# Chunked attention into a sine MLP on one core: four passes in another order of words, batch 3's loads issued elsewhere, the last output tile cut 384 and 128

## The chip, the core and the metric

The kernel runs on one core of a Trainium2 chip. The time is device microseconds of one execution of the whole program. A core has five instruction streams that run side by side and wait for each other by semaphores: PE (TensorE, matrix products; its weight loads are shown as PEld), DVE (VectorE), ACT (ScalarE), POOL (GpSimd) and SP (SyncE, which here only issues transfers). Each stream works through its instructions in the order in which the program was written, so an instruction that waits holds up all that stand behind it on its engine. ACT, POOL and SP also issue DMA transfers, which then run by themselves.

## What is computed

`reference.py`, cut to what matters. The attention works on chunks of 32 queries that see 16 keys to the left, 8 to the right and 8 memory rows:

```python
# q, k, v: (4, 8, 768, 64); mem_k, mem_v: (4, 8, 8, 64)
for c in range(768 // 32):
    ctx = slice(max(0, 32 * c - 16), min(768, 32 * c + 40))
    k_full = np.concatenate([mem_k, k[:, :, ctx]], axis=2)
    v_full = np.concatenate([mem_v, v[:, :, ctx]], axis=2)
    a = softmax(q[:, :, 32 * c:32 * c + 32] @ k_full.transpose(0, 1, 3, 2) / 8)
    out[:, :, 32 * c:32 * c + 32] = a @ v_full
x = out.transpose(0, 2, 1, 3).reshape(3072, 512)
h = x @ w_in                       # (3072, 2048)
g = h + sin(alpha * h) ** 2 / alpha
return g @ w_out                   # (3072, 512), float32
```

## The kernel before

Matrix operands are bfloat16, sums float32. The four batches (768 tokens each) pass through in five stages. Stage 0 is attention of batch 0; stage n (n = 1, 2, 3) runs the MLP of batch n-1 and, in between and after it, the attention of batch n; stage 4 is the MLP of batch 3. Only stages 1 to 4 differ in the change. One stage is one string of `WORDS`, written out by hand: `Stage.run` takes the words one by one, and the method for a word's first letter (`do_b`, `do_h`, ...) emits its instructions. So a word's place fixes its place on every engine at once, and an engine on which it emits nothing does not see it.

The MLP of a batch has 16 tiles of 128 of the 2,048 hidden columns:

- `b`*t* and `h`*t*: the two halves of tile *t*'s first product, four 384-column matmuls each (line 462) into two PSUM banks; `h` then has ACT take the sine (line 477)
- `q`*t*`A`, `V` or `P`: the square of the sine on ACT (line 482), DVE or POOL (line 485)
- `g`*t*: DVE's finish (line 489), which writes `gT` and gives the two banks back
- `o`*n*: puts the second product of this batch in the queue `feed`, 96 matmuls for six output tiles of 128 tokens; the first two tiles go together in groups of *n* hidden tiles. `f`*n* takes the next *n* of them (line 500, 512 columns each). After a tile's sixteenth, `close` copies it out of PSUM (line 507, ACT and DVE by turns as `e` says) and SP stores it (line 510). What is left at the end is taken in one go.

There are eight banks. `Banks` gives out pairs and singles in the order in which they were given back, so a `b` waits until an earlier tile's `g` has run.

The attention of a batch has eight blocks of 96 queries:

- `s`*jk..*: scores of these blocks (line 419, 16 matmuls of 96 columns for two blocks, 24 for three), then three exponentials each on ACT (line 433)
- `v`*j*: values (line 448, eight matmuls of 65 columns), then DVE's reciprocal and product (lines 387, 388)
- `t`*j* and `T`*j*: the block turned by PE (line 400) and copied to `xT` by DVE or ACT (line 403); `c`*j*: turned by a DMA transpose that SP issues (line 669)
- `V`*bxy*: POOL issues the loads of `v` of batch *b*, heads *x* to *y*-1 (lines 209, 216; float32 in memory, bfloat16 on chip, into buffer *b* mod 2, with the memory rows between); `m`, `H` copy the memory rows (DVE, or eight copies on POOL, line 232)
- `R`*n*: POOL issues the next *n* loads of the next batch's key rows (16, lines 269 and 275) and, after them, query rows (6, line 282); `Z`: SP adds the memory rows; `X`*n*: SP issues the next *n* DMA transposes of these into `kT` (8, line 297) and `qT` (6, line 300). Batches 2 and 3 come this way.
- Batch 1 comes by `dk`, `dq` (one load each), `k`, `l` (turned by PE, line 313) and `K`, `L` (copies, lines 324 and 333)
- `U`, `I`: loads of `w_out` and `w_in`; `Ws`, `We`: one-element sine or exponential on ACT, which brings the function table in ahead of use.

The word method and the queue of the second product:

Of the kernel before, what the change touches and what calls it, by code (L numbers as in the profile page):

```python
# [27 lines left out]
    ),  # L28
    (
# [5 lines left out]
    ),  # L35
    (
# [5 lines left out]
    ),  # L42
    (
# [5 lines left out]
    ),  # L49
    (  # L50
# [3 lines left out]
    ),  # L54
)

# [66 lines left out]
def kernel(  # L123
# [15 lines left out]
    d_model, d_ff = moe_w_in.shape  # L139
# [178 lines left out]
    def copier(eng):  # L318
        return {"A": nc.scalar.copy, "V": nc.vector.tensor_copy, "P": nc.gpsimd.tensor_copy}[eng]
# [176 lines left out]
    def second(i, gT, group=0):  # L496


        def mm(o, s, ft, c0=0, c1=d_model):
            nc.tensor.matmul(  # L500
                o[:, c0:c1], gT[:, ft, P * s:P * s + P], w_out_sb[:, ft, c0:c1],
                start=(ft == 0), stop=(ft == FT - 1),
            )

        def close(o, bs, s, c0=0, c1=d_model):
            o_sb = mlp.tile([P, d_model], F32, name="o_sb", bufs=3)
            copier(state["engines"][state["o"] % len(state["engines"])])(o_sb[:, c0:c1], o[:, c0:c1])  # L507
            state["o"] += 1
            banks.give(bs)
            nc.sync.dma_start(out[S * i + P * s:S * i + P * s + P, c0:c1], o_sb[:, c0:c1])  # L510

        order = []
        if group:
            order = [(s, ft) for h in range(0, FT, group) for s in range(2)
                     for ft in range(h, h + group)]
        order += [(s, ft) for s in range(2 if group else 0, NSUB) for ft in range(FT)]
        held = {}
        for s, ft in order:
            if i == B - 1 and s == NSUB - 1:
                if ft == 0:  # L520
                    for c0 in (0, 256):
                        o, bs = banks.single()
                        for f in range(FT):
                            mm(o, s, f, c0, c0 + 256)
                        close(o, bs, s, c0, c0 + 256)
                yield
                continue
            if ft == 0:
                held[s] = banks.single()
            mm(held[s][0], s, ft)  # L530
            if ft == FT - 1:
                close(*held.pop(s), s)
            yield
# [7 lines left out]
    class Stage:  # L541
# [63 lines left out]
        def do_o(self, a):  # L605
            feed.add(second(self.i, self.gT, int(a)), NSUB * FT, lambda: self.ready(int(a)))
# [244 lines left out]
    def const_s():  # L851
# [4 lines left out]
                     s=const_s, z=const_z)  # L856
# [37 lines left out]
```

## Time and profile before

| | us |
|---|---|
| three runs, median (lowest to highest) | 215.28 (214.47 to 216.2) |
| the profiled execution, its own time | 214.86 |
| its span | 212.7 |
| its granted TensorE clock | 1.0 |

The span is what the trace covers; the rest of the execution's time lies around it. Times in views of the profile are counted from the span's start. The stages stand in the trace as follows: stage 1 begins its MLP at about 23.7 us, stage 2 at 74.2, stage 3 at 120.6, stage 4 at 167.3, and the last stretch of line 500 begins at 189. A line of the groups reads: source line, engine, operation, result and inputs, tile sizes, count, busy time in all, mean ns of one, then the idle time of the engine ahead of these instructions with what ended it. In the chain of waits, a line is a start, a length and the work that the end of the program depended on at that time.

### The profile page before, as it was taken

To read this page: it belongs to the slowest core of one execution; us is meant where nothing else is said; L and a number is where in the kernel's file an instruction comes from. 1 tells how busy PE (TensorE), PEld (TensorE's weight loads), DVE (VectorE), ACT (ScalarE), POOL (GpSimd) and SP (SyncE) were. 2 spreads that over 40 slices of the span, in tenths; PEclk is the share of its full clock that TensorE was granted. 3 is DMA by queue.
4 is the path that set the end of the run, shared out by engine and by line. 5 is a ranking of instruction groups with operands and counts; after the bars stand their busy time and mean duration, and the time that the engine had idled before them with its cause. 6 is when DMAs were issued, how large, how long until landed. Compare 5 with 4: busy or idle time off the path is not lost.

```text
span 212.7 us, 4568 instructions
## 1 busy us (share of the span) xinstructions
PE 203.1 (95%) x1759; PEld 118.0 (55%) x1781; DVE 139.2 (65%) x210; ACT 143.5 (67%) x229; POOL 100.1 (47%) x142
## 2 busy tenths in 40 slices
PE   7799899999999999999999999999999999999994
PEld 7467655655455555554456555554455455554453
DVE  4888788998352669957675569896347187865010
ACT  2698798968838579978827298968755189891110
POOL 8998607497497395129893058582000022200000
PEclk9999999999999999999999999999999999999999
DMA  5999999999999999999997259999944400000312
GB/s 158 328 156 140 210 209 204 204 164 176 166 143 133 180 136 123 114 142 158 140 206 111 90 119 117 151 140 132 130 105 107 136 0 3 2 0 0 151 49 99
DMA packets 95853, 27.82 MB, mean 131 GB/s; under 512 B 84808, under 2 KB 92376, under 8 KB 95832
## 3 DMA queue, kind: packets, MB, share of 16 engines
q0 software_dynamic: 69152, 13.64, 92.4%
q1 hardware_dynamic: 25720, 12.68, 29.6%
q10 hardware_dynamic: 960, 1.21, 1.7%
q8 instruction: 14, 0.23, 0.6%
q14 instruction: 7, 0.06, 0.1%
HBM read 29.66 MB, written 6.29 MB: 169 GB/s over the span
## 4 chain that ended last, share of the span: by engine, by line
PE 72%; DVE 7%; DMA 7%; ACT 6%; issue 4%; POOL 2%; SPq 1%; DVEq 0%
PE ps L500 35%; PE ps L462 28%; DMA vw<-in_v_dram 4%; DVE gT L489 3%; DMA kq_f<-in_k_dram 3%; PE ps L448 3%; DVE s L485 2%; PE ps L419 2%; ACT u L477 2%; DVE x_blk L388 2%; PE ps L313 1%; PE ps L400 1%; ACT s L482 1%; ACT qT L333 1%; POOL vw L209 1%
## 5 line engine op out<-in xcount | busy, mean ns | idle before, releaser
L500 PE MATMUL ps<-w_out_sb,gT 128*128 128x512 bf16 (+1 forms) x382 | 86.9, 370 | 1.3 <-issue 0.3
L462 PE MATMUL ps<-xT,w_in_sb 128*128 128x384 bf16 x512 | 86.2, 326 | 0.7 <-DVE gT L489 0.2
L489 DVE SCALAR_TENSOR_TENSOR gT<-s,inv_alpha,ps 128x768 bf16<-128x768 f32 x64 | 63.0, 1011 | 12.5 <-ACT s L482 5.1
L462 PEld LDWEIGHTS <-w_in_sb 128*128 128x128 bf16 x512 | 49.6, 98 | 35.4 <-issue 2.1
L477 ACT ACTIVATE u<-ps,alpha_sb 128x768 f32<-128x768 f32 x64 | 56.6, 894 | 17.8 <-PE ps L462 15.9
L500 PEld LDWEIGHTS <-gT 128*128 128x128 bf16 x400 | 37.1, 98 | 37.2 <-DVE gT L489 0.2
L485 POOL TENSOR_TENSOR s<-u 128x768 f32<-128x768 f32 x11 | 17.4, 1581 | 68.3 <-ACT u L477 57.0
L433 ACT ACTIVATE pt<-ps,biasm 128x256 bf16<-128x256 f32 x72 | 27.2, 488 | 10.5 <-PE ps L419 10.5
L507 DVE COPY o_sb<-ps 128x512 f32<-128x512 f32 (+1 forms) x15 | 9.9, 669 | 27.6 <-PE ps L500 25.7
L485 DVE TENSOR_TENSOR s<-u 128x768 f32<-128x768 f32 x23 | 21.9, 953 | 7.4 <-ACT u L477 7.4
L482 ACT ACTIVATE s<-u 128x768 f32<-128x768 f32 x30 | 25.0, 841 | 0.5
L388 DVE TENSOR_TENSOR x_blk<-ps,rinv 96x512 bf16<-96x512 f32 x32 | 22.0, 687 | 1.1
L507 ACT COPY o_sb<-ps 128x512 f32<-128x512 f32 (+1 forms) x10 | 5.7, 572 | 22.6 <-PE ps L500 22.6
L387 DVE RECIPROCAL rinv<-ps 96x8 f32<-96x8 f32 x32 | 6.4, 199 | 13.7 <-PE ps L448 13.1
L209 POOL DMA_DIRECT2D vw<-in_v_dram x13 | 11.8, 909 | 5.8 <-PE ps L400 4.7
L216 POOL DMA_DIRECT2D vw<-in_v_dram x13 | 13.3, 1022 | 1.6 <-DMA vw<-in_v_dram 1.5
L269 POOL DMA_DIRECT2D kst<-in_k_dram x16 | 12.0, 749 | 2.7 <-DMA vw<-in_v_dram 1.7
L275 POOL DMA_DIRECT2D kst<-in_k_dram x16 | 11.5, 716 | 1.4 <-DMA vw<-in_v_dram 0.9
L448 PEld LDWEIGHTS <-pt 128*128 128x128 bf16 x192 | 8.1, 97 | 4.9 <-ACT pt L433 1.2
L282 POOL DMA_DIRECT2D q_bf<-in_q_dram x12 | 10.7, 907 | 0.0
L403 ACT COPY xT<-ps 128x384 bf16<-128x384 bf16 x10 | 4.9, 496 | 7.7 <-PE ps L400 7.7
L448 PE MATMUL ps<-vw,pt 128*128 128x65 bf16 x192 | 8.9, 193 | 0.4 <-DMA vw<-in_v_dram 0.4
(83 smaller groups left out, 139.0 us busy)
## 6 DMA issues: line engine op xcount, KB each, us to landing
out_dram<-o_sb SPq DMA_DIRECT2D x23, 256.0 KB, 2.7
q_bf<-in_q_dram POOLq DMA_DIRECT2D x12, 128.0 KB, 7.5
kq_f<-in_k_dram SPq DMA_DIRECT2D x3, 384.0 KB, 6.1
kq_f<-in_q_dram ACTq DMA_DIRECT2D x3, 384.0 KB, 8.2
w_in_sb<-in_moe_w_in_dram POOLq DMA_DIRECT2D x1, 1152.0 KB, 12.9
vw<-in_v_dram POOLq DMA_DIRECT2D x7, 128.0 KB, 8.0
vw<-in_v_dram POOLq DMA_DIRECT2D x8, 112.0 KB, 8.1
kst<-in_k_dram POOLq DMA_DIRECT2D x14, 64.0 KB, 5.8
```

Of the source, the lines that this page charges most:

```text
L209: nc.gpsimd.dma_start(vw[0:64, lo:c1, 0:D], win(vflat, a, n, 64))
L216: nc.gpsimd.dma_start(vw[72:128, c0:hi, 0:D], win(vflat, base + QW * c0 + 48, hi - c0, 56))
L388: nc.vector.tensor_tensor(out=x_blk[:].rearrange("p g e d -> p e g d"), in0=otv[0:QW, :, :, 0:D], in1=rinv[:].unsqueeze(3).to_broadcast([Q ...
L433: nc.scalar.activation(pt[:, 0:H * QW].rearrange("p (g e c) -> p g e c", g=2, e=4)[:, :, :, 32 * m:32 * m + 32], sc[:, :, 0:4 * QW].rearra ...
L448: nc.tensor.matmul(otv[:, e, hp, :], pt[:, QW * i:QW * i + P], vws[b % 2][:, 2 * hp + e, j, 0:D + 1],)
L462: nc.tensor.matmul(t["hT"][:, hf, 0:HALF], w_in_sb[:, kt, P * t["ft"]:P * t["ft"] + P], t["xT"][:, kt, HALF * hf:HALF * hf + HALF], start= ...
L477: nc.scalar.activation(t["u"][:], t["hT"][:, :, 0:HALF], ACTF.Sin, scale=alpha_sb[:, ft:ft + 1])
L482: nc.scalar.activation(s2[:], u[:], ACTF.Square)
L485: e.tensor_tensor(out=s2[:], in0=u[:], in1=u[:], op=ALU.mult)
L489: nc.vector.scalar_tensor_tensor(out=gT[:, ft, :].rearrange("p (e c) -> p e c", e=2), in0=t["s2"][:], scalar=inv_alpha[:, ft:ft + 1], in1= ...
L500: nc.tensor.matmul(o[:, c0:c1], gT[:, ft, P * s:P * s + P], w_out_sb[:, ft, c0:c1], start=(ft == 0), stop=(ft == FT - 1),)
L507: copier(state["engines"][state["o"] % len(state["engines"])])(o_sb[:, c0:c1], o[:, c0:c1])
```

## The change

In stages 1 to 4 the words stand in another order. Most are the same words; a few differ in the engine letter or the split of a count. What stands elsewhere or is different, by stage:

- Stage 1: `q6` from POOL to ACT, `q11` from DVE to POOL, `q15` from DVE to ACT; `L0` from ACT to DVE, `L1` from DVE to ACT, `K1` from DVE to ACT, `K3` from ACT to DVE; `T3`, `T7` become `t3`, `t7` (DVE copies); `U01` ahead of the loads of batch 1, all other early `U` ahead of `q7P`; `b2` ahead of `b6`; `f7 h14` becomes `h14 f5`.
- Stage 2: four `Ws` fewer, four `We` more; `V202` ahead of the last key-row and the query-row loads; `V268` from ahead of the POOL square to after it and after the first scores; `q12P`, `q14A` become `q12A`, `q14P`; `b11` ahead of `h7`.
- Stage 3: `R16`, `H3`, `R6` become `R22`, `H3`; `V305` from behind `V357` to ahead of `q2V`, behind `q3P`; `V357` from behind `q13P` to behind `q9P`; two of the three `Ws` ahead of the scores and the one behind them go, four `We` come; `q10V`, `q13P`, `q14A` become `q10A`, `q13V`, `q14P`; `c7` ahead of `v5`; `f24` at the end becomes `f26`.
- Stage 4: `q1`, `q3`, `q14` become `q1V`, `q3A`, `q14P`; `b3` ahead of `h4`; no `Ws`.

The last of the 24 output tiles was two halves of 256 columns, each with sixteen matmuls, a copy and a store; it becomes 384 and then 128 columns.

```diff
 (stage 1)
-        'o8 b0 h0 I7g q0V U69 U12 b1 h1 dq108 q1A b4 h4 b3 g0 h3 b6 g1 dk108 q4V g4 q3A b2 h2 h6 b5 h5 Ufg g3 '
-        'b7 q2V U01 U56 q6P h7 g2 q5A b10 U24 q7P g6 h10 b9 q10A g5 h9 U45 b8 h8 g7 g10 q8A q9V V158 b11 h11 '
-        'g9 b13 g8 h13 l0 l2 l3 L0A L2A q13P k2 q11V Ube b15 U9b g11 Uef g13 K2V h15 b12 q15V h12 q12A b14 '
-        'g15 f7 h14 V125 k1 k0 g12 l1 K1V k3 L1V L3A q14V K3A K0A V102 dy f9 g14 s61 f16 m1 s70 s3 f13 v0 f3 '
-        'v6 Z2 c6 f6 v3 f5 s542 T3 f10 T0 v4 f6 v2 f2 v1 c4 c2 f7 v7 f1 T1 f3 v5 Ws T7 f8 t5 '
+        'b0 I7g U69 h0 b1 q0V h1 q1A b4 U01 dq108 dk108 h4 g0 b3 h3 g1 b2 q4V q3A h2 o8 g4 U12 b6 h6 g3 q6A '
+        'q2V b5 h5 b7 h7 g2 b10 q7P q5A g6 U24 Ufg h10 U56 q10A U45 b9 V158 h9 g5 b8 h8 g7 b11 g10 q9V q8A '
+        'h11 b13 q11P g9 g8 h13 l2 q13P l0 L0V Ube L2A l3 U9b Uef g11 k2 K2V g13 b15 V102 h15 q15A b12 g15 '
+        'h12 f2 b14 q12A h14 f5 k1 g12 k3 q14V k0 l1 L3A K1A dy K3V L1A Z2 K0A f9 V125 s61 g14 f16 m1 s703 '
+        'f13 v6 f6 v0 We v3 f7 s542 c6 T0 f10 v4 f4 v2 f2 c2 Ws t3 v1 v7 c4 f8 T1 f5 t7 v5 f9 t5 '
 (stage 2)
-        'b0 o1 h0 b3 R2 q0V h3 b1 Ws q3A g0 g3 h1 q1V b2 R4 h2 q2A b5 h5 b4 h4 Ws g1 g2 q5V g5 b6 q4A h6 R8 '
-        'Ws g4 b8 q6A g6 h8 R1 b9 q8V h9 b7 q9A g8 h7 R3 V378 b11 h11 V226 b10 g9 R4 h10 V202 V268 q7V Ws '
-        'q10A f2 X8 q11A g7 f8 b12 h12 g10 g11 b14 h14 q12P g12 b13 h13 q13A g13 q14A f7 X6 Z3 b15 g14 h15 f7 '
-        'eV We s24 q15V f6 g15 f7 s05 s1 f1 m2 f14 v4 v1 f6 v0 f1 v2 f2 c4 f6 s63 s7 t1 f4 c2 v6 T0 f4 v3 f4 '
-        'v7 c7 v5 t3 f17 t5 T6 '
+        'o1 b0 h0 b3 h3 q0V b1 q3A R4 h1 b2 h2 g0 b5 g3 q1V g1 q2A h5 b4 g2 h4 q4A b6 q5V g5 h6 R8 b8 V202 g4 '
+        'q6A h8 g6 b9 R2 h9 R1 R3 b7 b11 R4 q8V q9A h7 g8 V226 h11 b10 g9 h10 q7V f9 g7 q11A g11 X8 q10A b12 '
+        'g10 h12 V378 q12A b14 g12 b13 h14 h13 q13A f5 g13 q14P X6 g14 b15 h15 f10 We Z3 q15V s24 g15 V268 '
+        'f13 s150 f5 eV m2 v4 f10 v2 v1 v0 We f15 s637 t0 f5 v5 f3 T1 c2 v3 We f4 c4 v7 We v6 T3 c7 f16 We t6 '
+        'f1 T5 '
 (stage 3)
-        'b3 R16 H3 Ws b0 h0 h3 b5 h5 Ws b1 q5A q0V g0 q3P R6 g3 X4 h1 Ws q1A b2 h2 X4 g5 g1 b4 h4 b6 q4A q2V '
-        'h6 X2 g2 b7 h7 b9 h9 X1 g4 X1 q6V b8 g6 X2 eV o1 h8 q7P g7 q8A b11 h11 q11A q9P b10 g9 g8 h10 b13 '
-        'g11 h13 q10V g10 b14 h14 b12 q13P V357 V305 h12 g13 q12V q14A f8 eAV b15 g12 h15 f6 g14 q15V s24 f16 '
-        'g15 f2 s103 f9 v4 v0 f3 f2 c4 v3 f2 c3 v2 f1 c2 f6 c0 s675 f10 v1 f4 c1 Ws f1 v7 v5 c7 v6 f2 c6 c5 '
-        'f24 '
+        'Ws b3 b0 h0 R22 h3 b5 q0V h5 H3 q3P b1 q5A X1 eV g0 X4 h1 g3 X2 q1A g5 b2 h2 b4 g1 h4 X1 V305 q2V b7 '
+        'g2 q4A b6 g4 h6 h7 b9 h9 q6V b8 g6 h8 q7P X2 b11 X4 g7 q9P q8A h11 q11A V357 b10 h10 o1 q10A g9 g8 '
+        'b13 g11 h13 b14 b12 g10 h14 h12 q13V f1 q14P g13 q12V f12 g12 b15 h15 g14 f8 s24 eAV q15V g15 f11 '
+        's103 f9 v4 v0 f4 c4 We v2 c0 f3 c2 v3 f6 c3 s675 f1 We We f4 v1 f9 v7 c1 f2 c7 v5 We v6 c6 c5 f26 '
 (stage 4)
-        'b2 h2 q2V b0 h0 b4 q0A g2 h4 b3 h3 g0 o2 b1 h1 Ws q3P b6 q4V q1A h6 g4 b8 h8 g3 b5 g1 q6A h5 q5A b7 '
-        'g6 h7 b11 q8P g8 h11 b10 g5 q7V h10 q10A q11P b9 h9 q9A g7 g11 b12 h12 b15 g10 q12A h15 g9 g12 b13 '
-        'h13 b14 q15A h14 g15 q14A q13V g14 g13 '
+        'b2 h2 b0 h0 b4 b3 q2V q0A g2 h4 h3 g0 q4V b1 q3A o2 g4 h1 b6 h6 b8 h8 q6A g3 q1V b5 q8P h5 g1 g6 q5A '
+        'b7 g8 h7 b11 h11 b10 g5 q7V h10 q11P g7 b9 q10A h9 g11 b12 q9A h12 g10 b15 q12A h15 b13 g9 q15A h13 '
+        'g12 b14 h14 q14P g15 q13V g13 g14 '
@@ second @@
             if i == B - 1 and s == NSUB - 1:
                 if ft == 0:
-                    for c0 in (0, 256):
+                    for c0, c1 in ((0, 384), (384, d_model)):
                         o, bs = banks.single()
                         for f in range(FT):
-                            mm(o, s, f, c0, c0 + 256)
-                        close(o, bs, s, c0, c0 + 256)
+                            mm(o, s, f, c0, c1)
+                        close(o, bs, s, c0, c1)
```

## The prediction

> **What bounds the kernel now.** I read the head of the page first, then the groups by shape, then the chain of waits.
>
> ```profile
> span 212.7 us, 4568 instructions
> PE 203.1 (95%) x1759; PEld 118.0 (55%) x1781; DVE 139.2 (65%) x210; ACT 143.5 (67%) x229; POOL 100.1 (47%) x142
> ```
>
> ```profile
> L462 PE MATMUL ps<-xT,w_in_sb 128*128 128x384 bf16 x512 | 86.2, 326 | 0.7 <-DVE gT L489 0.2
> L500 PE MATMUL ps<-w_out_sb,gT 128*128 128x512 bf16 x350 | 83.4, 379 | 1.3 <-issue 0.3 <-ACT qT L333 0.2
> L489 DVE SCALAR_TENSOR_TENSOR gT<-s,inv_alpha,ps 128x768 bf16<-128x768 f32 x64 | 63.0, 1011 | 12.5 <-ACT s L482 5.1 <-POOL s L485 4.4 <-DVE s L485 0.5
> L477 ACT ACTIVATE u<-ps,alpha_sb 128x768 f32<-128x768 f32 x64 | 56.6, 894 | 17.8 <-PE ps L462 15.9 <-DVE gT L489 1.4
> L482 ACT ACTIVATE s<-u 128x768 f32<-128x768 f32 x30 | 25.0, 841 | 0.5
> L485 DVE TENSOR_TENSOR s<-u 128x768 f32<-128x768 f32 x23 | 21.9, 953 | 7.4 <-ACT u L477 7.4
> L485 POOL TENSOR_TENSOR s<-u 128x768 f32<-128x768 f32 x11 | 17.4, 1581 | 68.3 <-ACT u L477 57.0 <-issue 11.3
> ```
>
> ```profile
> 23.73 0.49 PE ps L462 x3
> ...
> 41.25 0.81 PE ps L313 x24
> ...
> 66.45 0.17 PE ps L400 x4
> ...
> 74.17 10.44 PE ps L462 x64
> ...
> 107.74 0.48 PE ps L448 x16
> ...
> 143.70 8.88 DMA vw<-in_v_dram
> ...
> 154.47 0.24 PE ps L448 x8
> ...
> 156.89 0.62 PE ps L419 x24
> ...
> 160.01 1.08 PE ps L500 x5
> ...
> 209.66 0.37 ACT o_sb L507
> ```
>
> PE's 95% says little alone, because a matmul's duration overlaps the next one's; the chain's pieces give the pace. A 384-column matmul takes 10.44/64 = 0.163 us, a 512-column one 1.08/5 = 0.216, a score 0.62/24 = 0.026, a value 0.24/8 = 0.030, a transpose 0.81/24 = 0.034 at line 313 and 0.17/4 = 0.043 at line 400. From 23.73 on the order asks for 512 x 0.163 = 83.5, 368 x 0.216 = 79.5 (23 output tiles of 16; the table has 350 records, some are missing), 3.4 for the last tile (below), 192 x 0.026 = 5.0, 192 x 0.030 = 5.8, 96 transposes at line 313 (batch 1's) for 3.2 and 40 at line 400 (ten blocks) for 1.7: 182.1 us. The last copy starts at 209.66, so 185.9 us were there for it. **All that PE can win back after 23.73 is 3.8 us**, and part of that is the price of changing between long and short matmuls, which stays. The instructions before 23.73 do not change. So any order can win about 1.5% at the most, but can lose without limit.
>
> Two of these waits can be seen singly (PE and SP rows of the timeline):
>
> ```profile
> 150.18 2.12 PE L500 MATMUL ps<-w_out_sb,gT 128*128 128x512 bf16 x9
> 152.71 0.68 PE L448 MATMUL ps<-vw,pt 128*128 128x65 bf16 x16 [0.42 <-DMA vw<-in_v_dram]
> ```
>
> ```profile
> 165.67 1.25 SPq L669 DMA_TRANSPOSE xT<-x_blk  x1
> ...
> 167.26 2.05 PE L462 MATMUL ps<-xT,w_in_sb 128*128 128x384 bf16 x10
> ```
>
> Nine matmuls from 150.18 occupy PE until 152.12; the values start at 152.71: 0.59 us waiting for batch 3's last V load, issued at 143.70 and landed 8.88 later. Ten matmuls from 167.26 need 1.63, and 0.16 more until the last one's modelled end: 1.79, but took 2.05. The 0.26 is tile 2's second half waiting for the last block that SP transposes (issued 165.67).
>
> **The change part by part.**
>
> *V and query loads of batch 3.* These rows of POOL's timeline set the times:
>
> ```profile
> 94.59 1.46 POOL L485 TENSOR_TENSOR s<-u 128x768 f32<-128x768 f32 x1 [8.80 <-ACT u L477]
> 96.00 0.68 POOL L269 DMA_DIRECT2D kst<-in_k_dram  x1
> ...
> 108.81 4.49 POOL L232 COPY vw<-memv_st 8x512 bf16<-8x512 bf16 x8
> 124.63 1.46 POOL L485 TENSOR_TENSOR s<-u 128x768 f32<-128x768 f32 x1 [11.33 <-issue]
> 126.04 5.34 POOL L282 DMA_DIRECT2D q_bf<-in_q_dram  x6
> ...
> 140.75 0.87 POOL L209 DMA_DIRECT2D vw<-in_v_dram  x1
> ```
>
> POOL now idles 11.33 us after the eight memory copies, then squares tile 3 (124.63), then issues the six query loads. R22 puts those six (5.34 us) into the idle time. V305 then follows tile 3's square, from about 126 instead of 142.5, and V357 tile 9's square, a little before 140.75. Both land over 5 us before the values: **-0.6**, from 0 (if another wait stands there at once) to -0.6. What waits behind the early issues is tile 3's square: R22 starts at 99.5 (next paragraph), k loads take 12.8 (96.00 to 108.81), queries 5.3, copies 4.5: 122.1, 2.5 us before 124.63. Covered.
>
> *Batch 2's heads 6 and 7 (V268) go the other way*: now issued ahead of stage 2's only POOL square (94.59), they go behind q14P, which stands later in the stage than q12P did. From 74.17 PE does 14 and a half tiles of 8 x 0.163 and f9 (9 x 0.216) until tile 14 is complete: 95.0, plus 0.2 of stalls; sine 0.9 and handover 0.15: 96.2; square 1.46: 97.7. The two issues start at 97.7 and 98.6 and R22 follows at 99.5. The first values of batch 2 are at 107.74 now (chain); before them stand 42 instead of 52 L500 matmuls (f9 f5 f10 f13 f5 against f2 f8 f7 f7 f6 f7 f1 f14), so they come at 107.74 - 10 x 0.216 = 105.6. The landing must take under 7 us from 98.6. The nearest rows, same size, lie on both sides of that:
>
> ```profile
> vw<-in_v_dram POOLq DMA_DIRECT2D x1, 128.0 KB, 4.9
> ```
>
> ```profile
> vw<-in_v_dram POOLq DMA_DIRECT2D x2, 128.0 KB, 15.5
> ```
>
> The first (issued in 135 to 146) had nearly the DMA engines to itself once SP's transposes were over; the second (80 to 90) shared them with k and q transposes and four query loads. At 98 us the loads ahead of it are 20 us old, so I take 4.9: landed at 103.5, **0**. Bounds: 0 and 98.6 + 15.5 - 105.6 = 8.5.
>
> *Transposes of batch 3 (X).* On SP they follow the same stores and memory rows:
>
> ```profile
> 75.17 11.09 SPq L297 DMA_TRANSPOSE kT<-kst  x6
> 86.35 10.09 SPq L300 DMA_TRANSPOSE qT<-q_bf  x6
> ...
> 121.64 11.76 SPq L297 DMA_TRANSPOSE kT<-kst  x8
> 133.50 8.80 SPq L300 DMA_TRANSPOSE qT<-q_bf  x6
> ```
>
> At 1.47 us each for the eight and 8.80/6 for the last six, they end at 142.3. The first scores of batch 3 stand three scores (0.6), 18 L500 matmuls (3.9) and two scores (0.4) ahead of 150.18, at about 145.2. V305's 600 KB now move beside them, but the 768 KB of queries no longer do: **0**, from -0.3 to the third rival's price.
>
> *Squares and copies.* Stage 1: tile 6 moves POOL to ACT, 11 DVE to POOL, 15 DVE to ACT, so DVE loses 2 x 0.95 and ACT gains 2 x 0.84. Of the k/q copies two change places each way. I laid ACT and DVE end to end with the rows above (0.89 a sine, 0.84 or 0.95 a square, 1.01 a finish) from the stage's start. By the same laying-out of both orders, tile 10 still waits 0.3 for tile 2's finish. Tile 8 then waits about 0.15, because ACT's queue is one square longer. Tile 15 waits 0.5 for the bank of the first two turns (0.3 now). The wait of the matmuls behind the last turns (0.4 now) goes, because f5 stands between tile 14 and the turns. **Net 0**, bounds -0.7 and +1.0. Stage 2: tile 11 opens one half tile earlier (b11 ahead of h7), 0.1 us ahead of tile 6's finish; fewer no-op sine warm-ups on ACT give as much back: **0**, bounds -0.2 and +0.9. Stage 3: the first eight finishes stand on DVE in the same order, and that order carries the waits there, so they stay; q10 moves to ACT, q13 to DVE: **0**. Stage 4: tile 11's wait for tile 6 (ACT's sines and squares ahead of it are the same number) stays: **0**. The sine table is now loaded without a warm-up, but ACT is done with its last output copy 3.5 us before that stage: 0; without that cover the load would stand ahead of the stage's first sine.
>
> *Attention orders.*
>
> ```profile
> L433 ACT ACTIVATE pt<-ps,biasm 128x256 bf16<-128x256 f32 x72 | 27.2, 488 | 10.5 <-PE ps L419 10.5
> ```
>
> Stage 3: c7 goes ahead of the last two values and 26 L500 matmuls instead of 24 follow the last transpose: 0.43 us more for a wait of 0.26: **-0.26**. Tighter than now are v1 behind s675 (five L500 matmuls between instead of ten) and v4 behind s150 (five): 5 x 0.216 and the last two scores, 0.4, make 1.5 us from the first block's scores, and its three exponentials need 3 x 27.2/72 = 1.13 and some 0.2 of handover: 0, bounds 0 and +1.0.
>
> *Last tile.* Copies and store:
>
> ```profile
> 207.97 0.42 DVE L507 COPY o_sb<-ps 128x256 f32<-128x256 f32 x1 [4.51 <-PE ps L500]
> 209.66 0.37 ACT L507 COPY o_sb<-ps 128x256 f32<-128x256 f32 x1 [2.91 <-PE ps L500]
> ```
>
> ```profile
> L507 ACT COPY o_sb<-ps 128x512 f32<-128x512 f32 x9 | 5.3, 594 | 19.7 <-PE ps L500 19.7
> ```
>
> ```profile
> out_dram<-o_sb SPq DMA_DIRECT2D x2, 128.0 KB, 1.7
> ```
>
> The halves close 1.69 us apart, 0.106 a matmul. Sixteen 384-column matmuls cost 2.6 (0.163 each) and sixteen of 128 columns 0.053 each, 0.85: 3.45 against 3.4, nothing. The price of 128 columns is in no row; 65 columns with the same weight load cost 0.030 and 256 cost 0.106, so the bounds are -0.4 and +0.85. ACT's copy shrinks by 128 columns: (0.594 - 0.372)/2 = 0.11 us. Half the bytes may take 0.1 off the store's 1.7. DVE's copy of 384 columns begins 0.85 us before the end, takes about 0.42 + 0.11, and its store leaves first. **-0.2**.
>
> The Trainium skill ("TensorE: Matmul & The Clock Gate", section "Back-to-back issue gap") speaks against this piece: it gives a stream of weight loads and matmuls 81 ns each at 128 columns and 131 at 512. By it the last sixteen cost 1.30, and the sum would end 0.45 later. Here 512 columns take 216 and a 65-column pair 30, so the trace disagrees at both ends, and I keep 0.053.
>
> **The sum.** -0.6 - 0.26 - 0.2 = -1.05. The profiled execution took 214.86 (span 212.7 and 2.1 around it), so 213.8. That execution lies 0.4 under the median of 215.28 (214.47 to 216.2). About 1%, 2.15 us, is what a measurement of this kernel can tell from no change: under 213.1 is faster, over 217.4 slower.
>
> **Rivals.**
> 1. *The waits move and nothing is won.* With V there, the values wait for the exponentials of the same blocks, and the 384-column store lands last. For it: ACT's queue is full at that place; against it: the first block's exponentials need 1.3 us and nine L500 matmuls (1.9) stand between. 214.9.
> 2. *Most of the 3.8 us goes.* The looser places (26 matmuls, f5, tile 2 ahead of tile 6 in stage 1) also end stalls that I left in place: 3.8 less the 0.86 above leaves 2.9; I put 1.1 of it down to the changes between long and short matmuls, as an estimate. 213.8 - 1.8 = 212.0. Against it: DVE's order, which carries them, is mostly the same.
> 3. *V305 slows the transposes of batch 3.* At the pace of 75.17 and 86.35 (1.85 and 1.68) the twelfth starts at 121.64 + 8 x 1.85 + 3 x 1.68 = 141.5 and ends its issue at 143.2; landing some 4 us after the issue, it holds the scores from 145 to 147. 213.8 + 2 = 216. The skill ("DMA: Bandwidth & Descriptors", section "Issuing engines are not separate DMA queues") has transfers of all issuers interleave on the same engines, which is this mechanism; the slower rows at 75 to 96 agree. Against it: 600 KB replace 768.
> 4. *Slower: V268 lands late.* It decides from a landing of 7 us on; at 12 us PE waits 98.6 + 12 - 105.6 = 5.0: 218.8. For it: 15.5 in the second row. Against it: nothing is queued ahead on POOL's queue.
>
> **How the numbers follow.** My sum 0.46 (own range 213.0 to 214.7), rival 1 0.18, rival 2 0.18, rival 3 0.08, rival 4 0.10. Predicted is 213.8. The range 212.2 to 216.6 leaves out half of rival 2 and rival 4 (0.19) and takes in the bounds of the other terms singly. Faster: rival 2 and 0.06 of my sum, 0.24. Slower: rival 4 and half of rival 3, 0.14, with 0.02 for several bounds together: 0.16. Within 1%: 0.60.
>
> **What would show it.** Right: no idle time of PE at line 448 put down to a V load near 150; V305's rows on POOL near 126; the first stage-4 run of L462 without its 0.26; a last copy of about 0.26 us, with the closes 0.85 apart. Wrong: line 448 waiting for a V load near 105 (rival 4); ACT's exponentials late near 145 behind line 419 (rival 3); closes 1.3 apart (the skill's price); new waits of line 462 for finishes in stages 1 and 2. If the time is under 213, PE's waits at line 462 must have gone.

## The result, and the profile after

| | before | after |
|---|---|---|
| median of 17 executions each, us | 214.69 (213.34 to 216.49) | 217.94 (215.83 to 223.25) |
| the profiled execution, us | 214.86 | 216.38 |
| its granted TensorE clock | 1.0 | 0.992 |

The ratio after to before is 1.0104 (95% interval 1.0075 to 1.0132). It leaves out eight of the 17 executions after, which took 219.09 to 223.25 and lie over 1.5% above the fastest; the median of the other nine is 217.17. The change makes the kernel about 1% slower. Forecast was 213.8, about 0.5% faster; the range ended at 216.6.

The head of the page after and the group of the first product hardly differ from before, except at the end of the group's line: PE's idle time ahead of these matmuls went from 0.7 to 1.9 us, and what ended most of it is a DMA that writes `xT`. (All lines of the code stand one lower after: 462 is 461, and so on.)

```profile
span 214.3 us, 4575 instructions
...
L461 PE MATMUL ps<-xT,w_in_sb 128*128 128x384 bf16 x512 | 86.4, 326 | 1.9 <-DMA xT<-x_blk 1.2 <-DVE gT L488 0.5
```

The chain of waits after names the places. None of the `xT` pieces stood in the chain of before:

```profile
70.64 5.82 DMA xT<-x_blk
...
119.20 5.08 DMA xT<-x_blk
```

PE's rows after, where stages 1 to 4 begin:

```profile
24.33 0.65 PE L461 MATMUL ps<-xT,w_in_sb 128*128 128x384 bf16 x3
...
74.51 0.34 PE L399 MATMUL ps<-ident,x_blk 96*128 96x96 bf16 x4
75.55 0.81 PE L461 MATMUL ps<-xT,w_in_sb 128*128 128x384 bf16 x4 [0.71 <-DMA xT<-x_blk]
76.51 3.75 PE L461 MATMUL ps<-xT,w_in_sb 128*128 128x384 bf16 x22
...
122.49 1.47 PE L461 MATMUL ps<-xT,w_in_sb 128*128 128x384 bf16 x8
124.42 2.76 PE L461 MATMUL ps<-xT,w_in_sb 128*128 128x384 bf16 x16 [0.47 <-DMA xT<-x_blk]
...
169.20 3.04 PE L461 MATMUL ps<-xT,w_in_sb 128*128 128x384 bf16 x17
```

The same of before:

```profile
23.56 0.65 PE L462 MATMUL ps<-xT,w_in_sb 128*128 128x384 bf16 x3
...
74.01 6.22 PE L462 MATMUL ps<-xT,w_in_sb 128*128 128x384 bf16 x37
...
120.59 6.72 PE L462 MATMUL ps<-xT,w_in_sb 128*128 128x384 bf16 x40
```

Four turns from 74.51 take 0.17, so the matmul at 75.55 comes 0.87 late; four more take 0.65, so that at 76.51 comes 0.31 late; eight from 122.49 take 1.30, so that at 124.42 comes 0.63 late. (The middle one has no cause in its row; in the chain above, the `xT` that was issued at 70.64 lands at 76.46, just ahead of it.) Together these are **1.81 us at the starts of stages 2 and 3**, and nothing there before. From these rows (stage 4 of before starts at 167.26) the stages compare so:

| from start to next start | before | after | after without the three waits |
|---|---|---|---|
| stage 1 | 50.45 | 51.22 | 50.35 |
| stage 2 | 46.58 | 46.94 | 46.63 |
| stage 3 | 46.67 | 46.71 | 46.08 |

Stage 2's first wait falls at the end of the first row, its second in stage 2, the third in stage 3. Without them stage 3 is 0.59 shorter, as much as the V wait of before. Inside the stages, then, the new order of the MLP is worth nothing either way. The remaining 0.77 of after's later start (24.33 against 23.56) lies in code that the change does not touch; it is taken up at the end.

### The profile page after: what moved, and what is told of

It is laid out like the page before. It is cut to its first block, busy times and chain, and to the rows that moved or that the text cites. A ratio compares the mean times of both kernels' runs of the same rounds, so it can differ in the third digit from the quotient of the medians.

```text
span 214.3 us, 4575 instructions
## 1 busy us (share of the span) xinstructions
PE 204.2 (95%) x1759; PEld 118.3 (55%) x1781; DVE 138.3 (65%) x209; ACT 144.6 (67%) x231; POOL 99.4 (46%) x142
## 4 chain that ended last, share of the span: by engine, by line
PE 70%; DVE 11%; DMA 8%; ACT 4%; issue 4%; SPq 1%; DVEq 0%; ACTq 0%
PE ps L499 34%; PE ps L461 26%; DMA xT<-x_blk 5%; DVE gT L488 4%; DVE s L484 3%; DMA kq_f<-in_k_dram 3%; DVE x_blk L387 3%; PE ps L312 2%; PE ps L418 2%; PE ps L447 2%; ACT u L476 2%; ACT s L481 1%; DVE rinv L386 1%; PE ps L399 1%; ACT qT L332 1%
## 5 line engine op out<-in xcount | busy, mean ns | idle before, releaser
L499 PE MATMUL ps<-w_out_sb,gT 128*128 128x512 bf16 (+2 forms) x382 | 86.9, 370 | 1.3 <-issue 0.5
L484 POOL TENSOR_TENSOR s<-u 128x768 f32<-128x768 f32 x11 | 16.4, 1496 | 89.5 <-ACT u L476 71.8
L499 PEld LDWEIGHTS <-gT 128*128 128x128 bf16 x400 | 36.6, 98 | 37.8
L481 ACT ACTIVATE s<-u 128x768 f32<-128x768 f32 x31 | 26.0, 842 | 0.9
L506 ACT COPY o_sb<-ps 128x512 f32<-128x512 f32 (+1 forms) x11 | 6.2, 567 | 25.4 <-PE ps L499 25.4
L729 PE MATMUL ps<-zeros 128*128 128x128 bf16 x64 | 6.7, 278 | 1.4 <-DVE tiny L766 1.2
```

Source lines behind the costliest of these rows:

```text
L481: nc.scalar.activation(s2[:], u[:], ACTF.Square)
L484: e.tensor_tensor(out=s2[:], in0=u[:], in1=u[:], op=ALU.mult)
L499: nc.tensor.matmul(o[:, c0:c1], gT[:, ft, P * s:P * s + P], w_out_sb[:, ft, c0:c1], start=(ft == 0), stop=(ft == FT - 1),)
```

## The theories

**Theory A**: POOL's loads now run beside the DMA transposes that turn the last attention blocks of a stage, these land late, and PE waits for them at the next stage's start. The rows of the DMA issues, by window, after (66 to 74.5, then 112 to 121; the last number is the median from issue to landing, over those whose landing the trace has: of the `xT` in the first window, that is the last one alone):

```profile
q_bf<-in_q_dram POOLq DMA_DIRECT2D x6, 128.0 KB, 6.3
...
xT<-x_blk SPq DMA_TRANSPOSE x2, 5.8
...
q_bf<-in_q_dram POOLq DMA_DIRECT2D x6, 128.0 KB, 6.7
...
xT<-x_blk SPq DMA_TRANSPOSE x3, 5.6
```

And before, where the second window has no query loads:

```profile
q_bf<-in_q_dram POOLq DMA_DIRECT2D x2, 128.0 KB, 5.5
...
xT<-x_blk SPq DMA_TRANSPOSE x2, 3.5
...
xT<-x_blk SPq DMA_TRANSPOSE x2, 2.3
```

Why the loads moved is to be read in POOL's rows; before:

```profile
65.89 1.80 POOL L282 DMA_DIRECT2D q_bf<-in_q_dram  x2
72.40 0.69 POOL L209 DMA_DIRECT2D vw<-in_v_dram  x1 [4.71 <-PE ps L400]
...
76.65 3.55 POOL L282 DMA_DIRECT2D q_bf<-in_q_dram  x4
```

and after:

```profile
70.79 3.50 POOL L281 DMA_DIRECT2D q_bf<-in_q_dram  x4 [1.38 <-PE ps L499]
74.26 1.12 POOL L208 DMA_DIRECT2D vw<-in_v_dram  x1
...
98.08 1.46 POOL L484 TENSOR_TENSOR s<-u 128x768 f32<-128x768 f32 x1 [19.57 <-ACT u L476]
99.49 0.87 POOL L208 DMA_DIRECT2D vw<-in_v_dram  x1
...
112.93 5.28 POOL L281 DMA_DIRECT2D q_bf<-in_q_dram  x6
118.25 4.51 POOL L231 COPY vw<-memv_st 8x512 bf16<-8x512 bf16 x8
127.10 1.46 POOL L484 TENSOR_TENSOR s<-u 128x768 f32<-128x768 f32 x1 [4.34 <-issue]
```

In the order of before, `V378` (head 7 of batch 3's values, which goes into the buffer that batch 1's last values are still read from) stands ahead of `R4`, the last four query loads of batch 2. It waits 4.71 us for PE, and everything behind it on POOL's queue waits too: **the wait works as a gate**: POOL issues nothing from 67.7 to 72.4, while SP's two transposes go (issued from 68.44, the last landed at about 73.3). After, `V378` stands behind `R4`, and the loads are issued from 70.79, on top of the transposes (issued 69.30 to 71.9). The list of the change by stage does not name `V378`; the diff has it. At the end of stage 2 `R22` does the same with batch 3's six query loads.

**Theory B**: the order of tiles, squares and finishes inside stages 1 and 2 costs the time, and the waits at the stage starts are no more than where a late PE shows. Then undoing only POOL's moves would win nothing.

## The experiments

All were timed beside the kernel before, and the ratio given is to it. "Landing" is the median of `xT` in the windows 66 to 74.5 and 112 to 121, read as above.

**1. The last tile alone.** The kernel before with the 384 and 128 columns, no word moved.

```diff
-                    for c0 in (0, 256):
+                    for c0, c1 in ((0, 384), (384, d_model)):
```

> The kernel before with the last tile cut 384 and 128 and nothing else. Theory A (the loss is made at the starts of stages 2 and 3, where a DMA transpose of the attention's last blocks lands late because batch loads were moved beside it) and theory B (the loss is made inside the MLP passes by the other order of squares and tiles) both expect the prediction's 0.2 us less than before, with the last copy at about 0.26 us. If 128 columns with a weight load cost 81 ns, it is 0.2 us more than before instead.

Measured: 0.9982 (0.9956 to 1.0009), 214.69 against 215.33. The copies at the end stand as in the changed kernel (below). The interval includes no change, so a gain of some 0.4 is likely and not shown. Its profiled execution has neither the V wait near 152 nor the 0.26 at stage 4's start, though no word was moved: two of the three gains that the prediction summed come and go by themselves.

**2. The gate put back.** The changed kernel with `V378` ahead of `R4`.

```diff
-        'q6A h8 g6 b9 R2 h9 R1 R3 b7 b11 R4 q8V ... g10 h12 V378 q12A ...
+        'q6A h8 g6 b9 R2 h9 R1 R3 V378 b7 b11 R4 q8V ... g10 h12 q12A ...
```

> The changed kernel with V378 put back ahead of the last four query loads of batch 2, so that POOL again stops until batch 1's values are done. Theory A: the DMA transposes issued near 69 to 72 land in about 3.5 us again instead of 5.8, PE's 0.9 us at the start of stage 2 goes, and the time is 0.9 to 1.2 us under the changed kernel's. Theory B: no change within 0.3 us, the time stays about 1% over the kernel before.

Measured: 1.0073 (1.0036 to 1.0110). Landing 3.9 with two query loads in the first window, 6.4 with six in the second. PE's rows:

```profile
123.19 4.06 PE L461 MATMUL ps<-xT,w_in_sb 128*128 128x384 bf16 x24 [0.82 <-ACT tiny L742]
```

Stage 2 now starts without a wait, at 74.29; stage 3 still has one, of 0.98 in start times. (The profile names a one-element warm-up on ACT there, which ended just before. It is not what the matmul needs: in experiment 3 the same matmuls run past it. The block that SP turns last was issued at about 117.6 and landed 5.4 later, at 123.0.) In time the gain is within the intervals, so this run shows the place by its trace and not yet by its time.

**3. The query loads of batch 3 late again.** The changed kernel with `R16 ... q3P R6` instead of `R22`.

```diff
-        'Ws b3 b0 h0 R22 h3 b5 q0V h5 H3 q3P b1 ...
+        'Ws b3 b0 h0 R16 h3 b5 q0V h5 H3 q3P R6 b1 ...
```

> The changed kernel with batch 3's six query loads back behind tile 3's square (R22 split into R16 and R6), V305 still early. Theory A: the last DMA transpose of stage 2 lands in about 2.3 us instead of 5.1, the 0.63 us at the start of stage 3 goes, and the time is 0.6 us under the changed kernel's. Theory B: no change within 0.3 us.

Measured: 1.0054 (1.0031 to 1.0077). The opposite of experiment 2: landing 6.4 and 3.1, waits at stage 2's start of 0.42 and 1.32, none at stage 3's. But a wait of 0.98 came in at 138 to 139. POOL's rows, and DVE's and PE's behind them:

```profile
128.83 5.34 POOL L281 DMA_DIRECT2D q_bf<-in_q_dram  x6
134.11 1.28 POOL L208 DMA_DIRECT2D vw<-in_v_dram  x1
135.32 1.34 POOL L215 DMA_DIRECT2D vw<-in_v_dram  x1
136.61 2.96 POOL L484 TENSOR_TENSOR s<-u 128x768 f32<-128x768 f32 x2
```

```profile
138.19 1.01 DVE L488 SCALAR_TENSOR_TENSOR gT<-s,inv_alpha,ps 128x768 bf16<-128x768 f32 x1 [1.26 <-POOL s L484]
```

```profile
139.25 2.06 PE L461 MATMUL ps<-xT,w_in_sb 128*128 128x384 bf16 x11 [0.82 <-DVE gT L488]
```

Tile 7's square waits on POOL's queue until the eight issues are over, the finish waits for the square and PE for the bank. `R22` and the early `V305` belong together: with both early loads of V and the late query loads, POOL has 8 us of issuing ahead of a square.

**4. Turns by PE instead of DMA, placed together.** Blocks 2 and 4 of stage 1 and 7 of stage 2 turned by PE.

```diff
-        '... v2 f2 c2 Ws t3 v1 v7 c4 f8 T1 f5 t7 v5 f9 t5 '
+        '... v2 f2 Ws t3 v1 v7 f8 T1 t2 t4 f5 t7 v5 f9 t5 '
-        '... v6 T3 c7 f16 We t6 f1 T5 '
+        '... v6 T3 f16 We t7 t6 f1 T5 '
```

> The changed kernel with the DMA transposes that end stage 1 (c2, c4) and stage 2 (c7) done by PE with a DVE copy each instead; the loads stay where the change put them. Theory A: the waits of 0.88 and 0.63 us at the starts of stages 2 and 3 go, PE gets three times 0.17 us more work, so about 1.0 us under the changed kernel's, and the runs spread less. Theory B: 0.3 to 0.5 us over the changed kernel's, for the added work.

Measured: 1.0132 (1.0101 to 1.0162), no better than the change. It does not tell the theories apart. PE no longer waits for `xT` at the starts of stages 2 and 3, but turns that stand back to back wait for each other's copies, which I had not allowed for: three of them start 0.73, 0.69 and 0.61 late, 2.0 us in place of the 1.81. The first of them:

```profile
72.86 0.33 PE L399 MATMUL ps<-ident,x_blk 96*128 96x96 bf16 x4 [0.57 <-ACT xT L402]
```

**5. Both undone.** The changed kernel with 2 and 3 together, and `V305` behind `q9P`, so that tile 7's square goes first.

```diff
 (2 and 3, and)
-        '... b4 g1 h4 X1 V305 q2V b7 ... q9P q8A h11 ...
+        '... b4 g1 h4 X1 q2V b7 ... q9P V305 q8A h11 ...
```

> The changed kernel with V378 ahead of batch 2's last query loads, batch 3's query loads behind tile 3's square, and V305 behind tile 9's square, so that no long row of issues stands ahead of a square of POOL. All else of the change (the order of squares, tiles and attention, the last tile) stays. Theory A (the loss is made by loads in flight beside the DMA transposes that stages 2 and 3 begin with): both boundary waits go, and the time is 0 to 0.4 us under the kernel before. Theory B (the MLP order loses): still 0.5 to 1.0 us over the kernel before.

Measured: 1.0027 (0.9994 to 1.0061), 215.18 against 214.61: 0.0077 of the 0.0104 are gone, with nothing of the MLP's order undone. Theory A expected 0 to 0.4 us under the kernel before; the median lies 0.57 over it, and the interval includes no change. Landing 4.9 and 3.0; about 0.2 us of waiting for `xT` at the start of stage 2, none at stage 3's. Theory B would have kept the loss; it falls.

**6. V early in the kernel before.** Experiment 1 with `V305` moved ahead, behind `q9P`.

```diff
-        '... q9P b10 g9 g8 h10 b13 ... q13P V357 V305 h12 ...
+        '... q9P V305 b10 g9 g8 h10 b13 ... q13P V357 h12 ...
```

> The kernel before with the last tile cut 384 and 128, and V305 issued behind tile 9's square, ahead of V357, some 6 us earlier than now. If the 0.59 us wait for batch 3's V in the profile of before is there in every run, 0.6 us under the kernel with the new last tile alone; if it comes and goes with the landing times, 0 to 0.3 under it. About 0.2 to 1.0 us under the kernel before.

Measured: 1.0040 (1.0011 to 1.0069), where the same kernel without the move had 0.9982. The early V load is no gain, as expected, but a loss of about 1.2 us. The rows show 1.0 of it: q transposes land 8.0 after their issue in the window 130 to 147, with four V loads beside them, and the second half of the first scores starts 1.0 late.

```profile
vw<-in_v_dram POOLq DMA_DIRECT2D x1, 320.0 KB, 9.2
...
qT<-q_bf SPq DMA_TRANSPOSE x6, 8.0
```

```profile
147.67 0.35 PE L419 MATMUL ps<-qT,kT 64*128 64x96 bf16 x8 [0.88 <-DMA qT<-q_bf]
```

Before they land in 3.4 in that window, after in 5.0 (no wait), in experiment 5 in 8.3 (PE idle 0.23 for them at 147.21).

**7. `R22` alone in the kernel before.**

```diff
-        'b3 R16 H3 Ws b0 h0 h3 b5 h5 Ws b1 q5A q0V g0 q3P R6 g3 ...
+        'b3 R22 H3 Ws b0 h0 h3 b5 h5 Ws b1 q5A q0V g0 q3P g3 ...
```

> The kernel before with batch 3's six query loads issued right behind its key loads (R22) and nothing else. Theory A: the query loads are in flight when stage 2's last DMA transpose is, it lands in 5 to 6 us instead of 2.3, and PE waits 0.3 to 1.0 us at the start of stage 3: 0.3 to 1.0 us over the kernel before. Theory B: no change within 0.3 us.

Measured: 1.0036 (0.9997 to 1.0074). Landing in the second window 4.3 instead of 2.3, with three query loads in it (8.4 each). Stage 3 starts 0.54 late. The matmul's row puts that down to DVE's copy of an output tile, which ended at the same time; but that copy stands the same way in the kernel before, where the matmul does not wait for it. The row of its weight load (PEld) names `xT`:

```profile
121.57 1.42 PEld L462 LDWEIGHTS <-w_in_sb 128*128 128x128 bf16 x10 [0.53 <-DMA xT<-x_blk]
```

So the wait is Theory A's, and of the size that it expected; in time the interval still includes no change.

**8. The gate taken away in the kernel before.** `V378` behind `V268`, so that all six query loads go early.

```diff
-        '... g8 h7 R3 V378 b11 h11 V226 b10 g9 R4 h10 V202 V268 q7V Ws '
+        '... g8 h7 R3 b11 h11 V226 b10 g9 R4 h10 V202 V268 V378 q7V Ws '
```

> The kernel before with V378 moved behind the other loads of stage 2, so that POOL no longer stops at 67.7 for batch 1's values, and nothing else. Theory A: V226 and the last four query loads are in flight beside the two DMA transposes issued at 68 to 70, which land 2 us later, and PE waits 0.5 to 1.2 us at the start of stage 2: 0.5 to 1.2 us over the kernel before. Theory B: no change within 0.3 us.

Measured: **1.0259** (1.0213 to 1.0305), 220.38. One word moved in the kernel before costs more than the whole change, and far more than the 0.5 to 1.2 us expected: the landing grows by 4.4 us, not by 2. Its POOL row (the last four of the six), its landing (66 to 74.5) and PE's row at the start of stage 2:

```profile
70.54 3.53 POOL L282 DMA_DIRECT2D q_bf<-in_q_dram  x4
```

```profile
xT<-x_blk SPq DMA_TRANSPOSE x2, 7.9
```

```profile
78.24 2.08 PE L462 MATMUL ps<-xT,w_in_sb 128*128 128x384 bf16 x6 [3.53 <-DMA xT<-x_blk]
```

**9. The changed kernel again**, for a second trace.

> The changed kernel once more, for a second trace. Theory A (blocks turned by DMA land late at the starts of stages 2 and 3): 1.0 to 1.5% over the kernel before, with waits of line 461 for xT at one or both starts, 0.5 to 3 us in all, and landings of 5 us or more there. Theory B (the MLP's order inside the stages): the same time, but no such waits, and stages 1 and 2 longer by over 0.5 us inside.

Measured: 1.0124 (1.0076 to 1.0173), 217.88 against 214.99. Its profiled execution took 217.62, nearer to the median than the first one's 216.38, and the waits at the stage starts are larger:

```profile
L461 PE MATMUL ps<-xT,w_in_sb 128*128 128x384 bf16 x512 | 86.4, 326 | 3.3 <-DMA xT<-x_blk 2.7 <-DVE gT L488 0.3
```

```profile
122.81 1.47 PE L461 MATMUL ps<-xT,w_in_sb 128*128 128x384 bf16 x8
125.89 1.30 PE L461 MATMUL ps<-xT,w_in_sb 128*128 128x384 bf16 x7 [1.62 <-DMA xT<-x_blk]
```

By start times 0.86 + 0.53 at stage 2 and 125.89 - 122.81 - 1.30 = 1.78 at stage 3: 3.2 us, against 2.9 between the medians. Without these waits the stages take 50.34, 46.62 and 46.07, as in the first trace, so of the 1.5 us between the two spans 1.4 lie in the waits.

**10. `c7` ahead of the last two values**, in the kernel of experiment 1. Behind the last transpose stand 24 matmuls of the second product, as before, and not the 26 of the change.

```diff
-        '... f1 v7 v5 c7 v6 f2 c6 c5 f24 '
+        '... f1 v7 f2 c7 v5 v6 c6 c5 f24 '
```

> The kernel before with the new last tile and with the end of stage 3 as in the change (c7 ahead of two values, f24 last). If the wait of the last block turned by SP is there in most executions, 0.2 to 0.35 us under the kernel with the last tile alone; if it comes and goes, as the trace of that kernel suggests (none there), 0 to 0.2.

Measured: 0.9972 (0.9945 to 0.9999), 214.34 against 214.99: the lowest ratio here, 0.3% under the kernel before. Against experiment 1's 0.9982 the move is worth nothing that these intervals show.

**11. Turns by PE, set apart.** As 4, with matmuls of the second product between the turns.

```diff
-        '... v2 f2 Ws t3 v1 v7 f8 T1 t2 t4 f5 t7 v5 f9 t5 '
+        '... v2 f2 Ws t3 v1 v7 f6 t2 f4 T1 f4 t4 f2 t7 v5 f6 t5 '
-        '... v6 T3 f16 We t7 t6 f1 T5 '
+        '... v6 T3 f10 t7 f6 We t6 f1 T5 '
```

> The changed kernel with blocks 2 and 4 of stage 1 and block 7 of stage 2 turned by PE and copied, instead of by DMA, and with the turns set apart by matmuls of the second product. Theory A: no wait for a DMA at the starts of stages 2 and 3; 12 more transposes cost PE 0.5 us; so 0.3 to 0.6% over the kernel before. Theory B: the loss stays, 1% or more.

Measured: 1.0039 (1.0005 to 1.0073), with POOL's loads as in the change and twelve transposes more on PE. Stage 2 starts without a wait. My expectation that stage 3 would too was wrong: its blocks 2 and 4 still go by DMA, and beside the six query loads one now takes 9.07 to land:

```profile
74.78 5.53 PE L461 MATMUL ps<-xT,w_in_sb 128*128 128x384 bf16 x33
...
123.82 3.41 PE L461 MATMUL ps<-xT,w_in_sb 128*128 128x384 bf16 x20 [0.57 <-DMA xT<-x_blk]
```

```profile
114.61 9.07 DMA xT<-x_blk
```

Taking the blocks off the DMA transposes, without touching the loads, wins back 0.0085 of the 0.0124. That is the same cause removed from its other end.

**What they show together.** Landing beside the wait that it made at the start of stage 2: 3.2, 3.5 and 3.9 (experiment 1, before, 2) no wait; 4.9 (5) about 0.2; 5.8 (after) 0.87 + 0.31; 6.1 (9) 0.86 + 0.53; 6.4 (3) 0.42 + 1.32; 7.9 (8) about 3.7. At the start of stage 3, by the last block alone: 2.3 (before, 1, 3 and 5) none; 5.1 (after) 0.63; 5.4 (2) 0.98; 6.2 (9) 1.78. A later issue is not the reason: the last block of stage 2 goes out 4.5 us ahead of the first matmul that reads it before (117.39 to 121.89) and 4.6 after (119.20 to 123.79, by the pace). The loss goes when the loads are moved back (5), when the transposes are avoided (11), and comes when the gate alone is taken from the kernel before (8). Theory A is shown. That the transposes share the DMA engines with the loads is its reading of these landings; no run separates it from other ways in which a load could hold up a transpose. The 0.0027 that remain in 5 are within its interval and not traced further.

## Why the prediction was wrong, step by step

- **The bound of 3.8 us** held: no version won more than 0.65. The 1.1 us of it that rival 2 gives to changes between long and short matmuls is worked out from no row, and no run here shows it.
- **"V and query loads of batch 3"** is one of the two steps that failed. POOL's side came out as worked out: memory copies until 122.76, tile 3's square not delayed (4.34 us of idle time ahead of it), `V305` behind it at 128.5. The step asked who waits *on POOL* for the earlier loads, and for V's effect on the k and q transposes (rival 3). It did not ask which transfers are in flight at 112 to 119, where the loads now go: SP's transposes of stage 2's blocks, which stage 3's first matmuls need. "Covered" was true of an engine and not of the DMA engines. Cost: 0.63, 0.98 and 1.78 (after, experiments 2 and 9), sized at 0.
- **Batch 2's loads** are the other. The prediction followed `V268` and left out `V378`, which moves in the same stage. Its wait of 4.71 us stood in POOL's rows of before and read like slack. It was what kept four query loads away from the transposes; cost 1.2, 1.4 and 1.7 (after, experiments 9 and 3), and 2.6% where it was moved alone. The sum has no term for it.
- **-0.6 for V**: values no longer wait in the trace after, as forecast:

```profile
L447 PE MATMUL ps<-vw,pt 128*128 128x65 bf16 x192 | 8.6, 193 | 0.0
```

  But they also did not wait in experiment 1, with V where it was, so that this sign came out right says nothing for the move. A wait seen in one execution was taken for a constant. And the early V load has a price, rival 3's: 1.2 us in experiment 6.
- **Rival 4** (V268 lands late) fell: POOL's square ran at 98.08 and V268 went out at 99.49 (worked out: 97.7; the stage began late), and by the row above nobody waited for it.
- **Rival 3** had the right mechanism at the wrong place. The Trainium skill ("DMA: Bandwidth & Descriptors", section "Issuing engines are not separate DMA queues") has transfers of all issuers interleave on the same engines. This case agrees at three places: with POOL's loads beside them, landings grow from 2.3 to 5.1 and 3.5 to 7.9 (`xT`) and from 3.4 to 8.0 (`qT`). The prediction weighed it at the last of them alone.
- **MLP orders at 0** held: 50.45 and 50.35, 46.58 and 46.63, without the boundary waits, and 50.34 and 46.62 in the second trace. Experiment 5 keeps the new orders and is not shown to be slower than the kernel before.
- **-0.26 at stage 4's start**: the wait is not in the trace after, and not in experiment 1 either, where nothing of stage 3 was moved. It is the same mistake as with V. Experiment 10 finds no gain from the place of `c7`; the two more matmuls behind the last transpose were not tried alone.
- **Last tile -0.2** held in the trace:

```profile
210.57 0.56 DVE L506 COPY o_sb<-ps 128x384 f32<-128x384 f32 x1 [5.36 <-PE ps L499]
```

```profile
211.41 0.27 ACT L506 COPY o_sb<-ps 128x128 f32<-128x128 f32 x1 [2.91 <-PE ps L499]
```

  The copies start 0.84 apart, so 0.053 a matmul of 128 columns. The last copy takes 0.27 instead of 0.37, and the last store lands in 1.6 instead of 1.7. The Trainium skill ("TensorE: Matmul & The Clock Gate", section "Back-to-back issue gap") gives 81 ns a matmul at 128 columns, by which the copies would start an estimated 1.30 apart. This case does not agree. Experiment 1 puts the gain at 0.18%, within its interval.

So of the sum only the last tile came out near its size, its two waits came out at nothing, and the time was made by a term that was not in it: the late landing of blocks turned by DMA, 1.8 and 3.2 us at two stage starts in the two traces.

## What to carry to other kernels

When a load is moved, list what else is in flight where it goes, on every queue, and who waits for that first; an idle issuing engine says nothing about room on the DMA engines. An instruction that waits on an issuing queue also delays all that stands behind it, so before it is moved, ask what its wait was keeping away from what. And a wait of half a microsecond that hangs on a transfer's landing should be seen in a second execution before it is put into a sum.

## What the hardware showed that was not expected

- The landing of a DMA transpose of one 96-query block lies between 2.3 us with no load issued beside it (before, 117.39) and 9.1 beside six query loads (experiment 11), with the same 1.2 us of issue on SP in the median.
- In experiment 8 PE's wait of 3.7 us was followed by a lower granted clock (the third column from the end). It is 0.57 over the next four microseconds and 0.50 from 79 to 81, so some 3.4 us ran at one half and cost about 1.7 more. After the wait of 1.78 in experiment 9 the clock stayed at 1.0.

```profile
78.00:82.00 4.00, 3.76 (x14) 1.83 (x14) 0.07 (x1) 0.90 (x1) 2.08 (x3) 0.57 1.88 202
```

- The first trace of the changed kernel has such a stretch too, from 11.3 to 14.7, in code that both kernels share; its MLP starts 0.77 later than before's. In the traces with a mean clock of 1.0 that start lies anywhere from 23.11 (experiment 5) to 24.38 (experiment 1), so the 0.77 need not come from the clock. The trace of experiment 6, whose words are those of before up to stage 3, has it too (0.59 from 11 to 15), so it does not take the change. It does not make the loss either: in the session of experiment 9 the two executions of the changed kernel with a mean clock of 1.0 took 216.54 and 217.98, and the eighteen of the kernel before with 0.999 or more have a median of 214.76. What sets it off is open.
